# Two transformer layers on one core: one tile back to the plain product, some queries moved into the first tile, and new queue orders

## The chip, the cores and the metric

One core of a Trainium2 chip runs the kernel. The metric is the device time of one execution in microseconds (us); lower is better. The kernel has five instruction queues that matter here: TensorE (PE), VectorE (DVE), ScalarE (ACT), GpSimd (POOL) and SyncE (SP), which issues all transfers.

## The reference

Two layers, each a linear-attention block and an MLP, on 2048 tokens of width 512, in float32. Both layers use the same weights.

```
def _A_ref(x, wqkv, w_phi, wo):            # H = 32 heads of Dh = 16
    qkv = (x @ wqkv) -> q, k, v            # per head
    pq = q @ w_phi[h];  pk = k @ w_phi[h]
    phi_q = concat(softmax(pq), softmax(-pq))   # 32 features a head
    phi_k = concat(softmax(pk), softmax(-pk))
    kv = sum over s of phi_k^T v;  z = sum over s of phi_k
    o = (phi_q kv) / (phi_q z + 1e-6)
    return o @ wo

def _B_ref(x, w1, w2):                     # 512 -> 1792 -> 512
    return maximum(x @ w1, 0) @ w2

for each of two layers:
    x = x + _A_ref(layernorm(x), wqkv, w_phi, wo)
    x = x + _B_ref(layernorm(x), w1, w2)
```

## The kernel before, in words

**Numbers.** Every operand of a large product is split into two float16 halves, high and low, and each product of float32 matrices is three float16 matmuls (high by high, high by low, low by high: `PAIRS`). The weights are scaled, split once and stay on the chip.

**Chunks and tiles.** The 2048 tokens are 16 chunks of 128 (`NCH`) and 8 tiles of two chunks (`TT = 256`, `NT = 8`).

**The front of a layer.** For each chunk: normalise and transpose (`front_norm`, giving `xT`), the keys (`pk`, then the feature map: maxima and minima, differences, exponentials, sums and a product, over DVE, ACT and POOL), the values (`pv`), and `gather`, which adds to the state `kv`. The queries (`query`, `pq`, 12 matmuls) are copied from the bank to `qs` by ACT and stored in `q_dram`. Chunks that are not `direct` store `xT` in `xt_dram`, and their query loads it again as `xq`: in layer 0 the chunks 6 to 15, in layer 1 the chunks 2 to 15. For layer 1 the front of most chunks lies among the tiles of layer 0.

**The opening of a layer** (`opening`). Once `kv` is complete: `summary` makes the right-hand side `rhs`; then for the two chunks of tile 0 the numerators (`pn`), their transposes (`turn`, `tr_o`, `oT`), the projection back (`pw`), the second normalisation (`back_norm`, `tr_b`, `yT`). The queries that are left are emitted here in bank `h`, which has two buffers, in the order of emission; the hidden products of the tiles use bank `h` after them.

**A tile** (`tile_steps`) has seven steps, each for 256 of the 1792 hidden columns. In a step stand the hidden product (`ph`), the activation to `h`, and the output product (`py`) of a step three before it. Among the steps stand, by the table that `sides` makes, the work for later tiles: `look` loads a chunk's query again (`ql`), makes its feature map (`p_q`, last on POOL at L685) and turns it by a transposing transfer on SP (`pT`, L550); `numerators`, `turn`, `back_project` and the normalisation follow a few steps later. They use bank `n`, which has two buffers.

**Plain and by seven.** A hidden step in the plain form (`hidden`, L1308) is 24 matmuls of 256 columns. By seven (`hidden_by_seven`, L1232) it is a scheme of Strassen's kind: seven products instead of eight, 42 matmuls of 128 columns, between which ACT takes three copies `sn` out of the bank (L1245) and DVE makes two adds (L1251, L1256). It needs sums of the rows, made on POOL by `norm_by_seven` (four differences at L958, spreads at L539) and turned by `turn_by_seven` into the place of a weight that is free, and sums of the first weight's blocks. These, seven of them, are made in layer 0 by `sums_of_weight`: 4 loads, 4 operations on POOL (L1105), one on ACT (L1095), one on DVE (L1099), two stores to `s_dram`; each step by seven loads one again as `s` (L1190, 512 KB). `SEVEN` names the tiles by seven of each layer: in layer 0 the tiles 1 to 7, in layer 1 all. `SECOND` names those whose output product goes by seven too (layer 1, tiles 2 to 7); it needs the sums of the second weight, made in layer 0 by `sums_of_second` and loaded from `t_dram` by `load_seconds` into the places of `Wq`, `Wv`, of two more buffers `xT` and of `v`.

**What sets the order.** The program emits tasks with their dependences; buffers of one tag are given out in order of emission. Each of the five queues then has an order written out as a string in `ORDER`: a digit says how many of the tasks still waiting, in order of emission, are passed over. The numbers at `add` are a planner's durations; with the strings in place they don't change what each queue runs, only the order in which the program is written down.

Of the kernel before, what the change touches and what calls it, by code (L numbers as in the profile page):

```python
# [14 lines left out]
ALU = mybir.AluOpType  # L15
# [7 lines left out]
NCH = S // P  # L23
# [6 lines left out]
SEVEN = (range(1, NT), range(NT))  # L30
# [25 lines left out]
        "031110020100990377022b4448012284015183101480220822085130061820310G3003C306207232035q1061013510gg30e20c00"  # L56
        "a00071000020020100000137110001145021373012330201111111190000800000mp00000000p000000000000d00h0l000000000"
        "0000b000000000b0000011111110000000020000000000300030000000000000000050005d00b00f000000000b0000a000008000"
        "0000600000000000000000111100000300030000000000000007a00gg000j00m000000000g000000000000000490000000000000"
        "00000001111116110000300000000000000000003000020007060b00e0000d0000000f0000500000000000000000000011111111"  # L60
        "000011120000000000000000036000b0000000000011111122201122012223333344444444033344444444444444440333333302"
        "222222g2222222222201111111112211112222223331223333333333344444444403333344402222225222222i222l220n111111"
        "110000h00000000000000000242232322000f0010bb0aa008830605003106070009b000000000000000011011111122202222220"
        "1111000000002000001111100001100111111111100000g000g0000000000p0r0000000000p00000000000s00000000000L0000K"
        "00000000V000V0000000000000000000000000000000000000000000m000000000r000000P0000000000I000000V0000000R0000"
        "0000R0000000000000000000000000000000A000Z2000000000000000000000J000000000000000000000000E0000D000I000000"
        "0000000000000000A00000000000000000000000000E00000000000w0000000000000000000w0000000000p0000t000000000000"
        "000000p0000000000000000000000000000000000000000000000000000000000000000000000000000000000000000000000000"
        "0000000000000000000000000000000000000000000000000000000000000000000000000000000000000000000000000000",
    DVE:  # L70
        "331132010000e20c110002110020c0b0k01811922c70h3211d2111e1Yi1c00T0dR44e466f0a5H00ea03302j0w7h1100g00e000j0"
        "d77fb0600ad13ob31000H00efD0G000003H302n0m00k0j1211f111c11f1e1o2131l2p1j122l4f33111222222j1i221f423l11j1i"
        "311122100111525201ee105240311811671605908022040a3902060d2c01a1000013131152131000552772066514112144033908"
        "2060d2c21000700131311524138812007991671194841050b0a09010e020100800601313110102010022330144550440601403a0"
        "92010041b119111051112112112103502325201210504030999908807067b6091514313211100000003022601444133304882225"
        "11101060550036605004403024033101221221000000037302l0k00i00g01e10ci0h0gu01s0r00140000E0MDDK0J01211Z5016Z2"
        "000Y3050200001V02T0211P0115Zc50Za41007171Z2Za01Z80099121ZtZ1Zs91071Zn1908002Zo04dZle11Zi01000ZE0d0ZBZK1b"
        "1ZH01221ZC80Zr160580771g10f11l011i0110111e0d4101101008811h204f110110h11f01200d13229101008471600100b11091"
        "1f0100b01c22a1107110777110110110110100013121011010011010011010001311001101101101100010010",
    ACT:  # L80
        "0033121104642021092110ff5c0ab9a08e1d50551g0o43m0ab0p317m2c62y501C10l150iZjo4tnZf03361Za51108p2hh16ll4184"
        "412d2301gg01200iC081f01b0g0f1302312101aa1e0ee02hyhMx010I101I0q0L1020310203f142c1gb000c80096807o0e69q0300"
        "10l10c10a10811100f2420000001k503h360515003833000421100c122133121070a6004070252429000051230e1440028021142"
        "2201110140303030171151060220030201713013125140a30072114222201122403100a411b06009420620131807105111003022"
        "832253002110000504003032201048403062520120060200205003028222343330022115040034222227780b70a209d9c3bcbbb1"
        "aa008aa88a49730652444401625611373056766676014404377232322023200669100300504060501100044133020m0080102f01"
        "d01m0akaj00h8g8fl8k07ix70vv0003120J101G1R2200B120J14077E0Z370Z175050534334P04Z303214X040373Zs05P56a6Zl05"
        "03Zh444Zu3903322ZnZY0Zm2ZV1000126010ZZ30lZJ100ZW2002ZS2201331214002ZZz2c01ZZc3021ZZq1ZZ7038072d201302u01"
        "a002ZM222004u42021002222103030211302010Zv0220000423830013q02017130401011o3310100303220130200030262040a02"
        "22013026200504h411240020110h330220400200a10200040028221a130221150440001302010030222040022003302040022100"  # L90
        "22201302010022010030222040302003022141020113021000000",
    POOL:
        "1003050930409500905090506y016v90040570b0500790070070b051b0700700101102288827200hhh0g0c10d09bb10002705023"
        "101007j0618811020307210400004744002000111215110014163302221111011102001111104400017360244030010000021011"
        "11050400501302321121112200020011110003020400242321111022001cc4b40302633201003330010000003300000aaaabbm0l"
        "100002100l0k0mm000005p01001k0u0t18U1T00041Z100Y001Zs1100cZn0ZyZy02222201b101110ZZ490ZNd0700910060q500Zy8"
        "0300110n20111001102201110008000Zea000706011o10302031202011i00000220110009000b0591006601000610000f0221101"
        "044d0020d00001110a50006050400060111002211111551311111000000000000010000000000403200000000000001110000000"
        "0",
    SP:  # L100
        "010010002692bf21032470z79b26b1c60250n34303472me834j3j0x2303099r2brcF4066m1226jB30e56S1100308c9hj120823n2"
        "0y1d0110b40022012149111070004763256823g63825266244g02d2066216o1956b7c412b3482051hg443270214619567j59759p"
        "3938175433300662161a6df785436ba1629k7662ae41479022a67cee67b429113330706070a690860032304451bu1n51r411635m"
        "002c32T34fRC24a4w22a77JsF9sa879G196185Ag50eE6L7474hj0s633100a69Ffe9ep1H0c16db9a334H4O5949V27h17mX8628662"
        "50Z0412k21Z2p5141345345002211070g60302i46402221117045002464026222a00045002203323320110400244433001113300"
        "00010",
# [167 lines left out]
def tile_kernel(ctx: ExitStack, tc: tile.TileContext, x_in, wqkv, w_phi, wo, w1, w2, out):  # L274
# [757 lines left out]
    def activate_by_seven(ph, h, n):  # L1032
# [28 lines left out]
        add(POOL, 0.63, first, reads=[r], makes=[rf], after=after_r, **now)  # L1061
        add(POOL, 0.385, lambda: nc.gpsimd.tensor_add(block(1), block(0), rf.ap[:, 1, :]),
            reads=[(rf, None)], writes=[(r, 1)], **now)
        add(ACT, 0.534, hi, reads=[(r, None)], makes=h, **now)
        add(POOL, 0.385, lambda: nc.gpsimd.tensor_sub(rf.ap[:, 2, :], block(2), block(1)),
# [4 lines left out]
        add(POOL, 0.875, lambda: nc.gpsimd.tensor_sub(s.ap[1], rf.ap, s.ap[0]),  # L1070
# [7 lines left out]
    def sums_of_weight(j):  # L1078
# [29 lines left out]
        add(DVE, 1.195, low, reads=[b, s, parts[0]], makes=[parts[1]], lock=True)  # L1108
# [7 lines left out]
    def sums_of_second(j):  # L1116
# [27 lines left out]
        add(DVE, 1.195, low, reads=[b, s, parts[0]], makes=[parts[1]], lock=True)  # L1144
# [16 lines left out]
    def load_seconds():  # L1161

        for j in range(NP):
            if j < 4:
                W, i = (Wq, Wv)[j // 2], j % 2
                seconds[j] = r = Second([lambda h=h, W=W, i=i: flat(W.ap[i])[:, h * 1024:(h + 1) * 1024] for h in range(2)])
                add(SP, 0.47, lambda j=j, W=W, i=i: nc.sync.dma_start(
                    flat(W.ap[i]).rearrange("p (h n) -> p h n", h=2), t_dram[j].rearrange("h p n -> p h n")),
                    reads=[t_res[j]], writes=[(W, f"t{i}"), r], kb=512)
                continue  # L1170
            if j < 6:
# [42 lines left out]
    def hidden_by_seven(l, t, s):  # L1214
# [35 lines left out]
        def plus():  # L1250
            add(DVE, 0.30, lambda: nc.vector.tensor_tensor(at(3), at(1), saved(2), op=ALU.add),  # L1251
                reads=[(ph, 1), (sn, 2)], writes=[(ph, 3)], boost=10 ** 6)

        def both():
            wide = lambda t: t.ap[:, :2 * P]
            add(DVE, 0.43, lambda: nc.vector.tensor_tensor(wide(ph), wide(ph), wide(sn), op=ALU.add),  # L1256
                reads=[(sn, 0), (sn, 1)], writes=[(ph, 0), (ph, 1)], boost=10 ** 6)
# [135 lines left out]
    def leave(l, t, n):  # L1393
# [24 lines left out]
        def plus(x, o, i, y, op, fast, n):  # L1418
            e = DVE if fast else POOL
            add(e, 0.12 + n / 940 if fast else 0.14 + n / 523,  # L1420
# [159 lines left out]
    def sides(l, t):  # L1580
# [41 lines left out]
    def opening(l):  # L1622
# [12 lines left out]
        for c in range(NCH):  # L1635
# [11 lines left out]
        else:  # L1647
            load_seconds()
# [79 lines left out]
    for l in range(2):  # L1728
# [3 lines left out]
        for t in range(NT):  # L1732
            tile_steps(l, t)
# [50 lines left out]
```

## Time and profile before

| | us |
|---|---|
| median of 3 runs | 1000.62 |
| lowest, highest | 999.99, 1003.89 |
| the profiled execution | 1001.27 |
| its span, first to last instruction | 999.5 |
| busy PE, DVE, POOL, ACT in it | 960.4, 675.4, 644.9, 554.7 |
| mean granted clock of TensorE | 0.992 |

Lines of the profile read thus: a group has the line of the code, the engine, the operation, out<-in by the program's names, and the count, then its busy time and the mean of one in ns, then the idle time of its engine just before it and what ended that. A wait has who waited, for what, the total in us, how many times and the longest. A timeline row has the start in us, the length in us, and in brackets an idle time before it. "PE" is the matmuls, "PEld" the loads of weights, "SPq" the queue that issues transfers. The granted clock is 1.00 at full speed.

### The profile page before, as it was taken

Reading aid. Unit: us, or ns where it says so; the run is one execution under the profiler, and the core shown is the slowest. Engines: PE = TensorE matmul, PEld = TensorE weight load, DVE = VectorE, ACT = ScalarE, POOL = GpSimd, SP = SyncE. Lnnn points to the kernel's source line nnn. Section 1 sums busy time; section 2 is a strip of 40 time slices with the busy share of each in tenths; the row PEclk is TensorE's granted clock in tenths of the full one; section 3 lists DMA queues with packets and bytes.
Section 4 is the critical chain, followed back from the end, with each engine's and each line's share of the span. In section 5 each row is a group of like instructions: output and inputs, shape, how many; then the busy total and the mean of one; then the engine's idle time right before and its main releaser. Section 6 shows DMA issues by size and latency. Waiting matters only on the chain.

```text
span 999.5 us, 24139 instructions
## 1 busy us (share of the span) xinstructions
PE 960.4 (96%) x9630; PEld 658.6 (66%) x9630; DVE 675.4 (68%) x1368; ACT 554.7 (55%) x1090; POOL 644.9 (65%) x627
## 2 busy tenths in 40 slices
PE   6999999897999999999999999998999999999997
PEld 5555555574566666656666665546667889888996
DVE  5889899884676777677564556986787644553333
ACT  6898885553454645455334344555455646555553
POOL 1487885787376576657215244475577888898775
PEclk9999999998999999999999999999999999999999
DMA  8365777779769698877846553898999785965540
GB/s 308 136 200 129 193 225 213 176 187 196 198 160 225 180 196 216 189 217 165 182 153 149 177 172 87 268 251 222 233 250 218 204 170 144 207 173 150 155 150 32
DMA packets 257937, 186.30 MB, mean 186 GB/s; under 512 B 186144, under 2 KB 193312, under 8 KB 257824
## 3 DMA queue, kind: packets, MB, share of 16 engines
q1 hardware_dynamic: 257824, 184.76, 70.7%
q8 instruction: 75, 1.23, 0.5%
q14 instruction: 38, 0.31, 0.1%
HBM read 107.51 MB, written 32.51 MB: 140 GB/s over the span
## 4 chain that ended last, share of the span: by engine, by line
PE 74%; DVE 9%; DMA 7%; POOL 5%; ACT 3%; issue 2%; SPq 0%; DVEq 0%; POOLq 0%; ACTq 0%
PE ph L1232 21%; PE py L1340 14%; PE py L1381 8%; PE pk L621 8%; PE pv L621 7%; PE pw L621 6%; PE pq L621 5%; DMA s<-s_dram 2%; PE kv L759 2%; DMA pT<-p_q 2%; PE pn L887 1%; DMA yT<-n_b 1%; POOL p_q L685 1%; DVE fm_q L665 1%; DVE e_q L657 1%
## 5 line engine op out<-in xcount | busy, mean ns | idle before, releaser
L1340 PE MATMUL py<-w,h 128*128 128x512 f16 x840 | 215.2, 381 | 0.0
L1232 PEld LDWEIGHTS <-s 128*128 128x128 f16 x2520 | 163.1, 98 | 43.4 <-issue 5.9
L1245 ACT ACTIVATE sn<-ph 128x128 f32<-128x128 f32 x315 | 86.0, 274 | 180.6 <-PE ph L1232 179.1
L621 PEld LDWEIGHTS <-xT 128*128 128x128 f16 x840 | 80.7, 98 | 91.2 <-DMA xT<-n_a 0.3
L1232 PEld LDWEIGHTS <-w 128*128 128x128 f16 x1890 | 118.9, 98 | 16.8 <-issue 1.6
L1340 PEld LDWEIGHTS <-h 128*128 128x128 f16 x840 | 74.7, 98 | 57.7 <-issue 1.4
L1251 DVE TENSOR_TENSOR ph<-ph,sn 128x128 f32<-128x128 f32 x105 | 31.3, 299 | 118.4 <-PE ph L1232 55.1
L1232 PE MATMUL ph<-yT,s 128*128 128x128 f16 x1260 | 104.9, 219 | 3.6 <-DVE ph L1251 2.9
L674 POOL TENSOR_TENSOR e_k<-e_k,fm_k 128x1024 f32<-128x1024 f32 x30 | 60.8, 2027 | 72.6 <-ACT fm_k L670 72.5
L1232 PE MATMUL ph<-yT,w 128*128 128x128 f16 x1260 | 104.6, 219 | 0.0
L685 POOL TENSOR_TENSOR p_q<-e_q,p_q 128x1024 f16<-128x1024 f32 x32 | 70.9, 2216 | 26.5 <-ACT p_q L681 21.9
L685 POOL TENSOR_TENSOR p_k<-e_k,p_k 128x1024 f16<-128x1024 f32 x30 | 67.5, 2249 | 29.8 <-ACT p_k L681 29.8
L621 PE MATMUL pw<-wo_h,oT 128*128 128x512 f16 x256 | 81.2, 379 | 2.9 <-DVE dn L895 1.7
L1256 DVE TENSOR_TENSOR ph<-ph,sn 128x256 f32<-128x256 f32 x105 | 44.9, 428 | 55.7 <-PE ph L1232 55.0
L621 PE MATMUL pk<-wk_h,xT 128*128 128x512 f16 x256 | 81.4, 379 | 0.0
L621 PE MATMUL pv<-wv_h,xT 128*128 128x512 f16 x256 | 80.9, 379 | 0.0
L674 POOL TENSOR_TENSOR e_q<-e_q,fm_q 128x1024 f32<-128x1024 f32 x32 | 61.9, 1936 | 28.7 <-ACT fm_q L670 28.6
L621 PE MATMUL pq<-wq_h,xq 128*128 128x512 f16 x208 | 65.1, 379 | 1.7 <-ACT e_q L661 1.4
L621 PEld LDWEIGHTS <-oT 128*128 128x128 f16 x384 | 36.4, 98 | 44.2 <-DMA oT<-n_o 2.5
L1000 DVE SCALAR_TENSOR_TENSOR h<-ph,h 128x512 f16<-128x512 f32 x70 | 47.6, 681 | 20.4 <-ACT h L997 19.9
L997 ACT ACTIVATE h<-ph 128x512 f16<-128x512 f32 x70 | 41.4, 591 | 34.5 <-DVE ph L1256 31.8
L539 POOL TENSOR_TENSOR n_a<-xn_a,n_a 128x512 f16<-128x512 f32 x26 | 30.1, 1159 | 42.0 <-ACT n_a L536 27.0
(233 smaller groups left out, 2291.8 us busy)
## 6 DMA issues: line engine op xcount, KB each, us to landing
s<-s_dram SPq DMA_DIRECT2D x105, 512.0 KB, 4.5
q_dram<-qs SPq DMA_DIRECT2D x32, 256.0 KB, 3.4
ql<-q_dram SPq DMA_DIRECT2D x32, 256.0 KB, 4.2
xt_dram<-xT SPq DMA_DIRECT2D x26, 256.0 KB, 3.5
xq<-xt_dram SPq DMA_DIRECT2D x26, 256.0 KB, 3.9
xe<-in_A_x_dram SPq DMA_DIRECT2D x16, 256.0 KB, 4.0
x<-in_A_x_dram SPq DMA_DIRECT2D x16, 256.0 KB, 4.1
x_dram<-x SPq DMA_DIRECT2D x16, 256.0 KB, 3.3
```

Source lines behind the costliest of these rows:

```text
L539: add(POOL, 0.14 + n / 523, lambda: nc.gpsimd.tensor_sub(n16.at()[:, n:], src(), n16.at()[:, :n]), reads=[x], writes=[(n16, "l")])
L621: nc.tensor.matmul(pm.ap, xT.ap[:, a, k, :], W.ap[b][:, k, :], start=(k == 0 and i == 0), stop=(k == KC - 1 and i == 2))
L674: (nc.vector if fast else nc.gpsimd).tensor_tensor(e3, e3, sm.unsqueeze(2).to_broadcast([P, 2 * n, DH]), op=ALU.mult)
L685: (nc.vector if fast else nc.gpsimd).tensor_sub(p16.ap[:, 1, cols], ef, p16.ap[:, 0, cols])
L997: nc.scalar.activation(h[0].ap, at(), AF.Relu)
L1000: add(DVE, 0.607, lambda: nc.vector.scalar_tensor_tensor(h[1].ap, at(), 0.0, h[0].ap, op0=ALU.max, op1=ALU.subtract), reads=[ph, h[0]], wr ...
L1232: nc.tensor.matmul(at(r), weight_of(i, b, kk, s, summed), rows_of(y, i, a, kk), start=(first and kk == 0 and n == 0), stop=(kk == 1 and n ...
L1245: nc.scalar.activation(saved(i), at(2), AF.Copy)
L1251: add(DVE, 0.30, lambda: nc.vector.tensor_tensor(at(3), at(1), saved(2), op=ALU.add), reads=[(ph, 1), (sn, 2)], writes=[(ph, 3)], boost=10 ...
L1256: add(DVE, 0.43, lambda: nc.vector.tensor_tensor(wide(ph), wide(ph), wide(sn), op=ALU.add), reads=[(sn, 0), (sn, 1)], writes=[(ph, 0), (ph ...
L1340: nc.tensor.matmul(py.ap, h[a].ap.rearrange("p j t -> p (j t)")[:, cols], W2.at(b, fs[j], slice(0, D)), start=(s == j == k == 0), stop=(s ...
L1381: nc.tensor.matmul(py.ap[:, 256 * r:256 * r + 256], left[a], right[b], start=(s == 0 and r == 0 and k == 0), stop=(last and k == 2), skip_ ...
```

## The change

It has five parts.

1. `SEVEN` for layer 0 begins with tile 2: tile 1 takes the plain hidden product, and its normalisation the plain form.
2. The sums of the first weight are made at other steps: three in tile 0 and four in tile 1 instead of four and three.
3. `KEPT = (3, 4)`: the last three queries of layer 0 and the last four of layer 1 are no longer in the opening but at index 1 of the first steps of tile 0, in bank `n` instead of `h`.
4. `load_seconds` in layer 1 is emitted before tile 1 instead of in the opening, and the seven loads go to the places in another order: `Wv` takes 0 and 1, the buffers `v` take 2, `xT` takes 3 and 4, `Wq` takes 5 and 6.
5. All five strings of `ORDER` are replaced, and some durations of the planner: six of POOL are longer, two of DVE (L1099 and its like) are longer, two of DVE in the product by seven are shorter.

```
-SEVEN = (range(1, NT), range(NT))
+SEVEN = (range(2, NT), range(NT))
+KEPT = (3, 4)
...
     def load_seconds():
         for j in range(NP):
-            if j < 4:
-                W, i = (Wq, Wv)[j // 2], j % 2
+            if j in (0, 1, 5, 6):
+                W, i = (Wv, j) if j < 2 else (Wq, j - 5)
...
-            if j < 6:
+            if j > 2:
                 bufs = [tiles(fr, "xT", [P, 2, KC, P], F16, f"second_{j}_{h}") for h in "hl"]
...
         if l == 0 and t < 2:
-            for j, s in enumerate((1, 3, 5, 5) if t == 0 else (0, 1, 2)):
-                put0(s, 2, sums_of_weight, j + 4 * t)
+            for j, s in enumerate((2, 3, 5) if t == 0 else (1, 2, 3, 4)):
+                put0(s, 2, sums_of_weight, j + 3 * t)
+        if t == 0:
+            for i in range(KEPT[l]):
+                put(i, 1, query, NCH - KEPT[l] + i, "n")
...
-        for c in range(NCH):
+        for c in range(NCH - KEPT[l]):
             if not (direct(l, c) if l == 0 else c < CPT):
                 query(l, c, "h")
...
             for i in range(2):
                 W2.split(i)
-        else:
-            load_seconds()
...
         for t in range(NT):
+            if l == 1 and t == 1:
+                load_seconds()
             tile_steps(l, t)
...
-        add(POOL, 0.63, first, reads=[r], makes=[rf], after=after_r, **now)
+        add(POOL, 0.69, first, reads=[r], makes=[rf], after=after_r, **now)
...
-        add(DVE, 1.195, low, reads=[b, s, parts[0]], makes=[parts[1]], lock=True)
+        add(DVE, 1.4, low, reads=[b, s, parts[0]], makes=[parts[1]], lock=True)
```

The strings of `ORDER` are not shown. The one of PE has 1395 digits instead of 1452.

More of the change, by code (lines that the diff above doesn't have):

```diff
@@ L55 @@
     PE:
[L56 to L65, printed above, removed]
@@ new lines @@
+        "02000000010131004110000320041520100414004035010134017802884107126203401404413302222333331222222333033333"
+        "33302220100000000111222000000000600900000005000000001111122222222211122222201111122233333022222200000000"
+        "00111222010002017000900000000030000001111122222222211122222222222333403333333333022222222333033022222244"
+        "44403030010000111011122222022222222222122222222222333444444444444444444455566666666888880788888999aaabbb"
+        "bbcccc0b0aaaaaab0aaaaaaaaaaaaaa0990880706055500333333333333333022222333252222222233322223330223333333333"
@@ L1069, in activate_by_seven @@
         add(ACT, 0.42, hi_sums, reads=[(rf, None)], makes=[s], after=after_s, **now)
-        add(POOL, 0.875, lambda: nc.gpsimd.tensor_sub(s.ap[1], rf.ap, s.ap[0]),
+        add(POOL, 0.92, lambda: nc.gpsimd.tensor_sub(s.ap[1], rf.ap, s.ap[0]),
             reads=[(rf, None), (s, None)], writes=[(s, "l")], **now)
@@ L1143, in sums_of_second @@
         add(ACT, 1.052, hi, reads=[b, s], makes=[parts[0]])
-        add(DVE, 1.195, low, reads=[b, s, parts[0]], makes=[parts[1]], lock=True)
+        add(DVE, 1.4, low, reads=[b, s, parts[0]], makes=[parts[1]], lock=True)
         for h in range(2):
@@ L1250, in plus @@
         def plus():
-            add(DVE, 0.30, lambda: nc.vector.tensor_tensor(at(3), at(1), saved(2), op=ALU.add),
+            add(DVE, 0.27, lambda: nc.vector.tensor_tensor(at(3), at(1), saved(2), op=ALU.add),
                 reads=[(ph, 1), (sn, 2)], writes=[(ph, 3)], boost=10 ** 6)
@@ L1255, in both @@
             wide = lambda t: t.ap[:, :2 * P]
-            add(DVE, 0.43, lambda: nc.vector.tensor_tensor(wide(ph), wide(ph), wide(sn), op=ALU.add),
+            add(DVE, 0.40, lambda: nc.vector.tensor_tensor(wide(ph), wide(ph), wide(sn), op=ALU.add),
                 reads=[(sn, 0), (sn, 1)], writes=[(ph, 0), (ph, 1)], boost=10 ** 6)
```

83 lines of the change are left out of this document (43 added, 40 removed).

## The prediction

> **What bounds the kernel now.** I read the page first (busy shares), then the windows of 25 us and 5 us, the waits, and the timeline of the stretches where TensorE (PE) is not full.
>
> ```profile
> span 999.5 us, 24139 instructions
> ...
> PE 960.4 (96%) x9630; PEld 658.6 (66%) x9630; DVE 675.4 (68%) x1368; ACT 554.7 (55%) x1090; POOL 644.9 (65%) x627
> ```
>
> PE is busy for 960.4 of 999.5 us, so a change pays only by taking work from PE, by closing some of the other 39.1 us, or by raising the clock. The windows say where those lie (columns: stretch, its length, busy time of PE, PEld, DVE, ACT, POOL, granted clock, DMA share, GB/s):
>
> ```profile
> 0.00:25.00 25.00, 16.50 (x108) 13.73 (x109) 14.48 (x42) 16.89 (x37) 4.70 (x17) 1.00 0.85 307
> ...
> 75.00:100.00 25.00, 25.00 (x197) 12.71 (x194) 23.38 (x34) 22.00 (x29) 17.98 (x12) 1.00 0.53 130
> ...
> 175.00:200.00 25.00, 20.11 (x201) 13.96 (x200) 20.80 (x42) 13.26 (x20) 19.66 (x15) 0.93 0.71 176
> ...
> 225.00:250.00 25.00, 17.98 (x187) 12.23 (x186) 12.31 (x31) 8.88 (x19) 19.77 (x21) 0.87 0.90 195
> ...
> 975.00:1000.00 25.00, 17.66 (x211) 16.08 (x208) 8.81 (x16) 8.27 (x20) 12.61 (x18) 0.95 0.07 25
> ```
>
> The start (8.5 us idle) and the end (7.3 us) are not touched. 4.9 us are idle at 175 to 200, the opening and first tile of layer 0, and 7.0 us at 225 to 250, where its second tile begins. The waits of PE, for 160 to 300 us and for 600 to 720 us:
>
> ```profile
> PE pn L887 <- DMA pT<-p_q: 5.8, 2, 4.9
> PE tr_b L565 <- ACT xn_b L599: 3.2, 2, 1.8
> PE pw L621 <- DVE dn L895: 1.7, 1, 1.7
> PE ph L1232 <- DMA s<-s_dram: 1.2, 1, 1.2
> PE tr_o L565 <- DVE o L898: 0.8, 1, 0.8
> ...
> PE pq L621 <- ACT e_q L661: 1.4, 1, 1.4
> ...
> PE pq L621 <- DMA xq<-xt_dram: 0.3, 1, 0.3
> ```
>
> So the dearest wait is that of the numerators for a turned feature map (pT) in tile 1. On GpSimd and on the DMA queue it looks so (start, us, operation):
>
> ```profile
> 236.67 0.73 POOL L1105 TENSOR_TENSOR sums<-sums 128x256 f32<-128x256 f32 x1
> 237.35 0.73 POOL L958 TENSOR_TENSOR xn_b<-xn_b,ts 128x256 f32<-128x256 f32 x1
> 238.04 2.13 POOL L685 TENSOR_TENSOR p_q<-e_q,p_q 128x1024 f16<-128x1024 f32 x1
> ...
> 240.38 2.91 SPq L550 DMA_TRANSPOSE pT<-p_q  x1
> ...
> 245.39 1.54 PE L887 MATMUL pn<-rhs,pT 128*128 128x68 f16 x24 [4.89 <-DMA pT<-p_q]
> ```
>
> The reader is to see a queue, not a slow transfer: the feature map's last GpSimd step stands behind the sums of the first weight (L1105) and the differences for the seven products (L958); only then can its DMA start, and PE waits 1.2 us more for the next sum of weights (s), the row of the waits.
>
> **The change, part by part.**
>
> (a) Layer 0's tile 1 by the plain product. A plain step is 24 matmuls of 256 columns, a step by seven 42 of 128:
>
> ```profile
> L1308 PE MATMUL ph<-yT,w x216: 218/272/311, 182.5 to 218.3; 128*128 128x256 f16 x60, 128*128 128x128 f16 x48
> ...
> 211.86 2.78 PE L1308 MATMUL ph<-yT,w 128*128 128x256 f16 x24
> 214.48 1.46 PE L1340 MATMUL py<-w,h 128*128 128x512 f16 x6
> ...
> 231.60 0.50 PE L1232 MATMUL ph<-yT,s 128*128 128x128 f16 x6
> 231.93 0.50 PE L1232 MATMUL ph<-yT,w 128*128 128x128 f16 x6
> ...
> s<-s_dram SPq DMA_DIRECT2D x105, 512.0 KB, 4.5
> ```
>
> Start to start, 214.48 - 211.86 = 2.62 us against 7 x (231.93 - 231.60) = 2.31 to 2.35 us (0.33 is rounded), so 0.27 to 0.31 us more in each of 7 steps: +1.9 to +2.2 us on PE, which nothing hides; I take +1.9. What goes with it: 7 of the 105 loads of s; in norm_by_seven and turn_by_seven four differences on GpSimd (0.73 us each by the row of L958 above) and two spreads with their two turns; 21 copies sn on ScalarE and 14 adds on VectorE. None is on the path where PE is full; they stand in front of pT where it is not.
>
> (b) The sums of the first weight go from 4 in tile 0 and 3 in tile 1, wanted from tile 1's first step, to 3 and 4, wanted from tile 2's. Their GpSimd work is the largest group in 160 to 275 us:
>
> ```profile
> L1105 POOL TENSOR_TENSOR sums<-sums 128x256 f32<-128x256 f32 x28 | 23.3, 832 | 2.7 <-DMA sums<-in_B_w_dram 1.8
> ...
> SPq L550 <- POOL sums L1105: 26.8, 9, 6.2
> ```
>
> The second row is the DMA queue's own wait list for 180 to 260 us: turns (L550) held in order for 26.8 us while the sums ran. The work stays; its due time moves a tile later (tile 0 has its hidden products from 182.5 to 218.3 us, row of L1308), so it can be put behind pT. I count no term for it by itself: it is why (a)'s and (c)'s cover can be used.
>
> (c) Three queries of layer 0 leave the opening for steps 0 to 2 of tile 0, in the other bank. One is 2.59 us on PE:
>
> ```profile
> 129.74 2.59 PE pq L621 x12
> ...
> 25.00:160.00 135.00, 135.00 (x965) 71.55 (x964) 120.06 (x211) 116.93 (x177) 99.91 (x65) 1.00 0.62 180
> ```
>
> Each takes along its load of xq and the store of qs on SP, and the copy to qs on ScalarE; what it stores is read back tiles later. It joins two lines: the buffers xq, which the halves of the weight's sums hold until they are stored, and bank n, which it holds through its copy. PE waited for xq 0.3 us in all before, and 1.4 us once for a bank whose copy stood behind an exponential (rows above, 600 to 720); so between 0 and 1.4 us for each of the seven moved queries, 9.8 us at most. I take 0, as the load can be issued early and the copy is one instruction; the end is kept for the range. 7.8 us of PE work move from a stretch in which PE has no gap to one in which it has them. pT is late by 5.8 us in all; with 7.8 us more work ahead of those numerators on PE, and less ahead of their turn on GpSimd (a, b), I take the 5.8 us to go, and with them the 1.2 us for s (no s is read in tile 1 any more): -7.0 us. The wait of pw for dn (1.7 us, at 192, inside tile 0) can have a query in front of it: -1.7 us. The gap at 178 to 182 (tr_b, 3.2 us) can't, as step 0 comes after it, and stays.
>
> Is the opening shorter by those 7.8 us? In 25 to 160 us VectorE was busy for 120.1 us; in 127.2 us that would be 94%. At 75 to 100 us it ran at 23.38 of 25 (94%) and PE had no gap. So the cover may be just enough; between none lost and all 7.8 us lost I take 1.5 us: +1.5.
>
> (d) The clock. After the gap at 240 to 245 the matmuls were slow:
>
> ```profile
> 240.00:245.00 5.00, 0.49 (x9) 0.32 (x6) 3.24 (x4) 3.15 (x6) 4.54 (x5) 0.83 1.15 232
> 245.00:250.00 5.00, 3.42 (x38) 2.94 (x39) 1.61 (x6) 0.38 (x2) 3.05 (x5) 0.50 1.03 269
> 250.00:255.00 5.00, 5.00 (x30) 2.66 (x28) 3.24 (x8) 2.01 (x4) 1.06 (x2) 0.65 0.56 124
> ...
> 180.00:185.00 5.00, 3.66 (x40) 3.65 (x41) 4.12 (x8) 3.41 (x5) 3.21 (x2) 0.69 1.01 249
> ```
>
> Lost: 0.49 x 0.17 + 3.42 x 0.50 + 5.00 x 0.35 = 3.5 us, which go with the gap: -3.5. The 3.66 x 0.31 = 1.1 us after the gap at 178 to 182 stay with it.
> The Trainium skill ("TensorE: Matmul & The Clock Gate", Part 1: The HAM clock gate) says that the array drops to half rate after an idle window of about 3.4 us and needs about as long of work to come back. By that page, as an estimate, one such gap costs some 1.7 us, and the sum would end 1.8 us higher. The 5 us rows show more after the 4.89 us gap, and a drop at 180 where no gap was over 1.82 us, which the page's window would not give; the rows decide.
>
> (e) Layer 1: four queries to steps 0 to 3 of its first tile, and the loads of the second weight's sums (t_dram) behind them, since two lie in Wq.
>
> ```profile
> 606.00:640.00 34.00, 34.00 (x245) 17.71 (x244) 27.20 (x51) 16.93 (x27) 13.64 (x9) 1.00 0.64 184
> 640.00:676.00 36.00, 33.30 (x251) 16.96 (x248) 30.32 (x62) 18.90 (x29) 22.71 (x17) 1.00 0.97 252
> 676.00:700.00 24.00, 21.11 (x239) 14.97 (x238) 16.13 (x37) 12.00 (x28) 13.35 (x10) 1.00 0.81 224
> 700.00:725.00 25.00, 25.00 (x269) 16.62 (x266) 18.79 (x46) 12.79 (x27) 14.43 (x13) 1.00 1.10 238
> ```
>
> The opening, 606 to 676, has 67.3 us of PE work and 57.5 of VectorE's. Without 4 x 2.59 = 10.4 us PE has 56.9, so VectorE sets it: at the 94% above 61.2 us, 8.8 less than 70. Tile 0 gains 10.4 us of work and loses its 2.9 us of gaps (24.00 - 21.11), which the queries can fill. Together -8.8 + 10.4 - 2.9 = -1.3 us. Bounds: the opening not shorter at all, +7.5; as short as PE allows, 56.9, -5.6.
>
> (f) New orders for all five queues, and costs that only feed the planner. Where the order of the rest of the work changes I can't price it from rows; the waits there, outside the places above, are some 5 us, of which I take nothing, and I leave the same on the other side.
>
> Sum: +1.9 - 7.0 - 1.7 + 1.5 - 3.5 - 1.3 = -10.1 us. The profiled execution took 1001.27 us (span 999.5), so 991.2; the median of the runs is 0.65 us lower, so 990.5.
>
> **The rivals.**
>
> 1. The openings don't get shorter (slower). The queries were the cover of a chain on VectorE, and the chain ends where it did; the moved PE work is added behind it. For: VectorE was busy for 89% and 84% in the rows of 25 to 160 and 640 to 676 us, where looks and weight splits stand in one queue with that chain. Against: PE had no gap at all at 94%. Price: 7.8 instead of 1.5 in layer 0, +7.5 instead of -1.3 in layer 1, which is 15.1 more, 1005.6; with one clock loss of the size of (d), 3.5, as the new gaps are long, 1009. It decides from the point where VectorE's share of an opening stays what it was, 89% in layer 0 and 57.5 of 70 us in layer 1.
>
> 2. The late transfers only move. The pT wait reappears in tile 1, or, as four of the seven sums are now made in tile 1, at tile 2's first s; and of t_dram's loads 1.25 MB (three of 256 KB, one of 512) were issued before 700 us and now come after, at the 238 GB/s of the row 700 to 725 5.3 us of transfer where the DMA share is 1.10 already.
>
> ```profile
> L1181 SPq DMA_DIRECT2D v<-t_dram x2: 479/524/570, 661.1 to 677.9; - x2
> L1181 SPq DMA_DIRECT2D second_h<-t_dram x2: 422/610/797, 678.5 to 706.4; - x2
> ...
> L1167 SPq DMA_DIRECT2D wq_l<-t_dram x1: 529/529/529, 692.7 to 692.7; - x1
> ```
>
> If the 5.8 us and their 3.5 us of clock stay, 990.5 + 9.3 = 999.8; if only the 5.3 us are added, 995.8. No change. Against it: the row 700 to 725 has no PE gap in spite of its share.
>
> 3. The new order also closes the other gaps: tr_b and tr_o (4.0 us) with their 1.1 us of clock, the 1.5 us of (c), layer 1 at its lower bound (4.3 more): 990.5 - 10.9 = 979.6. For: that much is idle. Against: these are chains, and PE needs something ready in them.
>
> **How the numbers follow.** Chances: the forecast (985 to 995.6) 0.50, rival 3 0.16, rival 2 0.20, rival 1 0.14. What a measurement can tell here is 0.5%, 5 us, so faster is below 995.6: 0.50 + 0.16 = 0.66, same 0.20, slower 0.14. The predicted time is the forecast's, 990.5; its own range is 985 to 995.6. Rival 3's time and rival 1's without the clock loss bound the whole range: 980 to 1005, which leaves out about 1 in 10 on each side.
>
> **What would show it.** In the new profile: no wait of pn for pT over 1 us between 200 and 300 us and a granted clock of 1.00 in the rows there (c, d); PE L1308 x384 instead of x216 and s loaded 98 times (a); the first step of tile 0 of layer 0 earlier by some 6 us than 182.5 and that of layer 1 earlier against the kernel's own 606 by some 9 us (c, e); DVE at over 90% in the openings. Wrong would make me: PE gaps with VectorE as releaser in 130 to 180 or 620 to 670 us (rival 1), waits for s at tile 2 or for t_dram's tiles after 725 (rival 2).

## The result and the profile after

| | us |
|---|---|
| changed kernel, median of 4 runs (lowest to highest) | 989.03 (988.47 to 990.29) |
| kernel before, on the same chip, median of 4 runs | 1002.25 (999.99 to 1008.23) |
| ratio, 95% interval | 0.9861 [0.9814, 0.9907] |
| the profiled execution of the changed kernel, its span | 990.29, 988.6 |

The changed kernel is faster by 1.4%, more than the 0.5% that can be told from no change. In the code after the change each line number is one less than before: L1307 is the plain hidden product, L1231 the one by seven.

First the page of the changed kernel.

```profile
span 988.6 us, 23825 instructions
...
PE 956.5 (97%) x9504; PEld 654.5 (66%) x9504; DVE 675.3 (68%) x1354; ACT 546.9 (55%) x1067; POOL 637.9 (65%) x621
...
s<-s_dram SPq DMA_DIRECT2D x98, 512.0 KB, 4.4
```

And from a list of one line's instructions the plain product (count, shortest, median and longest in ns, first and last start).

```profile
L1307 PE MATMUL ph<-yT,w x384: 216/272/273, 174.3 to 269.6; 128*128 128x256 f16 x144, 128*128 128x128 f16 x48
```

The change did what it says: 126 matmuls fewer (7 steps of 24 for 7 of 42), 384 plain ones, 98 loads of s. Now the windows that answer to those of before.

```profile
25.00:160.00 135.00, 134.76 (x991) 71.98 (x990) 118.94 (x212) 114.62 (x174) 97.00 (x65) 1.00 0.59 172
160.00:200.00 40.00, 36.56 (x350) 23.83 (x349) 36.27 (x72) 23.05 (x33) 25.10 (x17) 1.00 0.75 193
...
225.00:250.00 25.00, 25.00 (x194) 15.59 (x192) 14.02 (x36) 11.46 (x17) 23.08 (x25) 1.00 0.78 189
...
600.00:700.00 100.00, 95.91 (x851) 56.52 (x850) 77.56 (x155) 50.99 (x96) 56.65 (x42) 1.00 0.87 235
```

PE is full where 7.0 us were idle (225 to 250), at a clock of 1.00. The stretch around the first tile's start has come forward, so for it the window is 160 to 200 us in both kernels; in the kernel before it reads:

```profile
160.00:200.00 40.00, 34.34 (x342) 22.20 (x339) 34.92 (x72) 21.37 (x31) 28.74 (x22) 0.96 0.70 188
```

There 3.4 us are idle (40.00 - 36.56) where 5.7 were. Idle PE went from 39.1 us (999.5 - 960.4) to 32.1 (988.6 - 956.5). Busy PE fell by 3.9 us. Before, PE worked for 3.41 and 6.96 us in the two stretches in which the clock stood at 0.50 (the last section shows how they are found), so half of that, 5.2 us, was lost; after, it had no such work, so the work itself grew by 1.3. Together -7.0 - 5.2 + 1.3 = -10.9 us of span. The waits of PE from 150 to 310 us, all that are left:

```profile
PE tr_b L564 <- ACT xn_b L598: 1.2, 1, 1.2
PE ph L1307 <- ACT yT L569: 0.7, 1, 0.7
PE tr_o L564 <- DVE o L897: 0.7, 2, 0.3
PE tr_o L564 <- DVE dn L894: 0.5, 1, 0.5
PE ph L1307 <- DVE yT L573: 0.5, 1, 0.5
```

No wait for pT, s or dn in front of pw is among them. The queue, in the timeline of the same places as before:

```profile
226.59 5.20 POOL L684 TENSOR_TENSOR p_q<-e_q,p_q 128x1024 f16<-128x1024 f32 x2
231.75 0.55 POOL L601 TENSOR_TENSOR stat_a<-stat_a,nhalf 128x1 f32<-128x1 f32 x1
232.27 2.21 POOL L1104 TENSOR_TENSOR sums<-sums 128x256 f32<-128x256 f32 x3
...
231.81 2.96 SPq L549 DMA_TRANSPOSE pT<-p_q  x1
```

and the numerators of 180 to 260 us, from the list of instructions that touch pT:

```profile
L886 PE MATMUL pn<-rhs,pT x120: 192/194/198, 185.3 to 241.1; 128*128 128x68 f16 x120
```

The last GpSimd step of both maps of the pair now stands directly ahead of three operations of the sums; before, an operation of the sums and a difference stood directly ahead of the late one. The last turn is issued at 231.81 (240.38 before), and the last of the numerators starts at 241.1, well behind it.

Where does each layer end? The last hidden product by seven of a layer is the best mark (the second row of each pair is for layer 1):

```profile
L1232 PE MATMUL ph<-yT,w x168: 219/219/219, 500.3 to 606.6; 128*128 128x128 f16 x168
...
L1232 PE MATMUL ph<-yT,w x672: 218/219/219, 676.4 to 986.0; 128*128 128x128 f16 x168
```

for the kernel before, and for the changed one

```profile
L1231 PE MATMUL ph<-yT,w x132: 219/219/219, 504.8 to 595.0; 128*128 128x128 f16 x132
...
L1231 PE MATMUL ph<-yT,w x672: 217/219/219, 652.4 to 975.0; 128*128 128x128 f16 x168
```

Layer 0 ends 606.6 - 595.0 = 11.6 us earlier. Before, 12 matmuls of values (pv) more and 6 of the output product (py) fewer stood ahead of that mark, which makes 6 of 128x512, 1.3 us by the row of a query (2.59 / 12 each). So layer 0 is 10.3 us shorter and layer 1 (379.4 + 1.3 against 380.0) 0.7.

### The profile page after: what moved, and what is told of

Its sections match the earlier page's. It is cut to its first block, busy times and chain, and to the rows that moved or that the text cites. A ratio compares the mean times of both kernels' runs of the same rounds, so it can differ in the third digit from the quotient of the medians.

```text
span 988.6 us, 23825 instructions
## 1 busy us (share of the span) xinstructions
PE 956.5 (97%) x9504; PEld 654.5 (66%) x9504; DVE 675.3 (68%) x1354; ACT 546.9 (55%) x1067; POOL 637.9 (65%) x621
## 4 chain that ended last, share of the span: by engine, by line
PE 78%; DVE 7%; DMA 6%; POOL 3%; ACT 3%; issue 3%; SPq 0%; DVEq 0%; ACTq 0%; POOLq 0%
PE ph L1231 19%; PE py L1339 15%; PE py L1380 9%; PE pk L620 7%; PE pv L620 7%; PE pw L620 7%; PE pq L620 5%; PE ph L1307 4%; PE kv L758 2%; PE pn L886 2%; DMA oT<-n_o 1%; DMA ql<-q_dram 1%; DMA pT<-p_q 1%; DMA q_dram<-qs 1%; POOL p_q L684 1%
## 5 line engine op out<-in xcount | busy, mean ns | idle before, releaser
L1339 PE MATMUL py<-w,h 128*128 128x512 f16 x840 | 212.9, 379 | 0.0
L1231 PEld LDWEIGHTS <-s 128*128 128x128 f16 x2352 | 151.4, 98 | 37.5 <-issue 7.3
L1244 ACT ACTIVATE sn<-ph 128x128 f32<-128x128 f32 x294 | 80.2, 273 | 138.5 <-PE ph L1231 136.9
L1231 PEld LDWEIGHTS <-w 128*128 128x128 f16 x1764 | 110.8, 98 | 17.6 <-DVE h L999 2.7
L1250 DVE TENSOR_TENSOR ph<-ph,sn 128x128 f32<-128x128 f32 x98 | 29.3, 299 | 111.1 <-PE ph L1231 53.3
L1231 PE MATMUL ph<-yT,s 128*128 128x128 f16 x1176 | 97.6, 219 | 5.3 <-DVE ph L1250 2.9
L1231 PE MATMUL ph<-yT,w 128*128 128x128 f16 x1176 | 97.6, 219 | 2.1 <-DVE h L999 1.8
L673 POOL TENSOR_TENSOR e_q<-e_q,fm_q 128x1024 f32<-128x1024 f32 x32 | 64.9, 2030 | 35.7 <-ACT fm_q L669 35.7
L1255 DVE TENSOR_TENSOR ph<-ph,sn 128x256 f32<-128x256 f32 x98 | 41.9, 428 | 46.1 <-PE ph L1231 45.3
L620 PEld LDWEIGHTS <-xq 128*128 128x128 f16 x312 | 29.9, 98 | 35.5 <-DMA xq<-xt_dram 0.9
```

The lines of the kernel that those rows point to most:

```text
L620: nc.tensor.matmul(pm.ap, xT.ap[:, a, k, :], W.ap[b][:, k, :], start=(k == 0 and i == 0), stop=(k == KC - 1 and i == 2))
L673: (nc.vector if fast else nc.gpsimd).tensor_tensor(e3, e3, sm.unsqueeze(2).to_broadcast([P, 2 * n, DH]), op=ALU.mult)
L1231: nc.tensor.matmul(at(r), weight_of(i, b, kk, s, summed), rows_of(y, i, a, kk), start=(first and kk == 0 and n == 0), stop=(kk == 1 and n ...
L1244: nc.scalar.activation(saved(i), at(2), AF.Copy)
L1250: add(DVE, 0.27, lambda: nc.vector.tensor_tensor(at(3), at(1), saved(2), op=ALU.add), reads=[(ph, 1), (sn, 2)], writes=[(ph, 3)], boost=10 ...
L1255: add(DVE, 0.40, lambda: nc.vector.tensor_tensor(wide(ph), wide(ph), wide(sn), op=ALU.add), reads=[(sn, 0), (sn, 1)], writes=[(ph, 0), (ph ...
```

## The experiments

The experiments fall into three sets; in each, the kernel before ran between the others on the same chip (medians 1002.22, 1003.74 and 1003.5 us), and the ratios are to it. Two theories of the gap at 240 us stood against each other first: that pT is late by its place in the queues (A), or that the tile by seven itself is too tight (B).

**again**: the kernel before, unchanged.

> The kernel before, unchanged, for a second trace. If the late feature map belongs to the kernel, the wait of pn for pT at the start of the second tile of layer 0 (4.9 us) and the clock of about 0.5 behind it are there again, and the time is that of before within 0.3%. If they belong to the one execution, the wait is under 2 us here, and the sum of the prediction rested on a chance.

1.0007 [0.9987, 1.0027]. The gap is a property of the kernel: the longest wait for pT is 5.2 us (4.9 in the first profile). The clock loss after it was 3.0 us in this execution (half of the 5.96 us of work at 0.50), and none came at 180.

**late_map_first**: the late map's steps passed forward in three queues (parts of the strings of `ORDER`).

```
 ACT  -  ...1503h360515003833000...        +  ...1503h3g6051500333000...
 POOL -  "101007j0618811020307210400...     +  "101007j7i01881102030210400...
 SP   -  ...9111070004763256...            +  ...9111070a00463256...
```

> The kernel before with four instructions moved in its queues: the feature map of chunk 7 of layer 0 has its last step on ScalarE (high), its last two chunks' steps on GpSimd (low of chunks 6 and 7) and its turn on SP ahead of the normalisation for tile 2 and the sums that stood in front. Theory A, the queue: the late pT was only a matter of what stood in front of it; the 5.8 us of waits and the 3.5 us of clock go, the normalisation and the sums come some 4 us later and are not missed: 8 us faster (6 to 10). Theory B, the structure: the work in front is needed there, so the wait passes to s, to the rows of tile 2 or to a later map, and the gain is under 2 us.

0.999 [0.9972, 1.0008]. The waits of PE, 160 to 300 us:

```profile
PE ph L1232 <- DMA s<-s_dram: 4.1, 2, 3.3
PE pw L621 <- DMA oT<-n_o: 3.0, 1, 3.0
PE tr_b L565 <- ACT xn_b L599: 2.4, 2, 1.4
PE ph L1232 <- ACT sn L1245: 1.9, 2, 1.3
PE tr_o L565 <- DVE o L898: 0.8, 1, 0.8
```

The wait for pT is gone and its time stands at s, oT and sn. Theory A falls for this order: another place in the queues only hands the delay on.

**filler**: 20 matmuls of 128x512 whose result nobody reads, ahead of the late numerators.

```
+        if l == 0 and t == 1:
+            pb = bank("kv0", "filler")
...
+                for i in range(FILL):      # FILL = 20
+                    nc.tensor.matmul(pb.ap, Wk.ap[0][:, 0, :P], Wk.ap[0][:, 0, :], start=True, stop=True)
```

> The kernel before with 20 matmuls of 128x512 that nobody reads (20 x 0.216 = 4.3 us) put on TensorE in front of the numerators of chunk 7, in a bank that is free there; they fill the 4.9 us gap. Nothing else changes. By the rows of the granted clock (0.50 and 0.65 behind the gap) 3.5 us come back: 0.3 to 0.4% faster. By a window of some 3.4 us at half rate it would be 1.7 us. If the low clock has another cause than the gap, nothing.

0.9974 [0.9955, 0.9992]: 2.6 us faster with 4.3 us (20 x 2.59 / 12) of useless work, the interval 0.8 to 4.5. The clock after the gap:

```profile
240.00:245.00 5.00, 3.65 (x37) 1.86 (x35) 3.08 (x5) 1.36 (x4) 4.84 (x5) 1.00 1.02 188
245.00:250.00 5.00, 3.54 (x20) 1.90 (x21) 2.14 (x6) 1.31 (x2) 1.11 (x2) 0.70 1.12 303
250.00:255.00 5.00, 5.00 (x38) 2.88 (x36) 3.89 (x10) 2.52 (x5) 2.45 (x3) 0.96 0.57 183
```

The loss in these rows is 3.54 x 0.30 + 5.00 x 0.04 = 1.3 us, against 3.5 in the prediction's rows (1.7 by the recorded clock of the last section). So the time of a gap's slow clock is real, and cover on PE buys part of it back. This one profile took 1001.64 us (the median is 999.41) and has a second loss, at 421 us, that the kernel before doesn't have there. Over all executions the mean granted clock agrees: its median is 0.997 in 12 of filler and 0.993 in 28 of the kernel before.

**before_new_order**: the kernel before with all five strings found anew by a search over the planner's durations.

> The kernel before, the same instructions, with all five queue orders searched anew from its own (single tasks moved, a planner's durations as the measure, two more sets of durations beside the kernel's). If the new orders alone bring the gain of the change, 8 us or more here; if the tile by the plain product and the moved queries bring it, under 4 us.

1.0082 [1.0049, 1.0114]. A searched order is 8 us worse than the one written down, with the idle time spread out: 6.06 us at 160 to 200, 1.82 at 200 to 225, 3.82 at 225 to 300, 6.66 at 300 to 500. The wait for pT is down to 0.5 us in 160 to 300, with the same instructions; but PE waits there 2.9 us for oT and 1.8 for s. So this order too hands the delay on, as late_map_first does. Orders found by search must be compared with each other, not with an order that was there.

**sums_light**: the kernel before without the 28 operations on GpSimd of the sums.

```
-            add(POOL, 0.686, lambda o=o, x=x, y=y, f=f: nc.gpsimd.tensor_tensor(f32()[:, o], ...
+            add(POOL, 0.686, lambda: None, writes=[b])
```

> The kernel before without the 28 operations on GpSimd that make the sums of the first weight (the halves are made from the blocks as loaded, so the hidden products of the tiles by seven are of other weights); all transfers, conversions and orders stay. 28 x 0.83 = 23.3 us of GpSimd's time leave 165 to 265 us. If GpSimd's queue is what made pT and s late, the waits of the second tile go with it and 7 us of idle time and 3.5 of clock with them: 8 to 10 us faster. If the transfers are (SP's queue and the DMA share of 0.9 there), less than 3 us.

1.0023 [1.0004, 1.0041], and the gap stays. The wait of PE, 160 to 300 us:

```profile
PE pn L887 <- DMA pT<-p_q: 5.6, 2, 5.1
```

and the late map in the timeline:

```profile
235.26 1.05 ACT L681 ACTIVATE p_q<-e_q 128x1024 f16<-128x1024 f32 x1
...
237.89 2.13 POOL L685 TENSOR_TENSOR p_q<-e_q,p_q 128x1024 f16<-128x1024 f32 x1
238.06 3.10 SPq L1091 DMA_DIRECT2D sums<-in_B_w_dram  x4
...
241.26 2.95 SPq L550 DMA_TRANSPOSE pT<-p_q  x1
```

The prediction read GpSimd as the head of the queue. With those operations gone the map's step on GpSimd still comes at 237.89: its ScalarE half comes only at 235.26, behind copies sn and the halves of the normalisation by seven, and two differences follow it on GpSimd (236.40 and 237.21). It ends at 240.02, and the turn still waits until 241.26 behind four loads on SP. Read so, the chain goes through ScalarE's order, GpSimd's differences and SP's order; that the sums' operations are not its limit is shown.

**The parts apart.** The next five are the changed kernel with queries put back into the openings or not; the stretches of the order that an edit touches were searched anew, and `after_searched` is the control with no edit.

**after_searched**: only strings of `ORDER` in the openings and first tiles.

> The control for the two others: the changed kernel with nothing undone, its order searched again in the same stretches and by the same measure. If the search by itself costs nothing, the changed kernel's time, 988 to 991; what it has more is the price of the search, to be taken off the two others.

**kept1_only**: `-KEPT = (3, 4)` `+KEPT = (0, 4)`; layer 0 searched.

> The changed kernel with the three queries of layer 0 back in the opening, in bank h (KEPT = (0, 4)); the tile by the plain product, the sums' steps and layer 1 as changed. The order is the changed kernel's, with the tasks of layer 0's opening and its first two tiles searched again for the moved queries. If those queries were the cover that the late feature maps needed, some of the waits come back: 3 to 7 us slower than the changed kernel, 992 to 996. If the plain tile and the later sums were enough, 987 to 991.

**none_kept**: `+KEPT = (0, 0)`; both layers searched.

> The changed kernel with none of the seven queries moved (KEPT = (0, 0)), its order searched again in the two openings and the tiles behind them. The sum of the prediction puts the queries of layer 1 at 1.3 us and counts on those of layer 0 for the cover: 994 to 999. If the moved queries are worth little and the plain tile is what counts: 988 to 993.

**kept0_only**: `+KEPT = (3, 0)`; layer 1 searched.

> The changed kernel with layer 1's four queries put back into its opening; layer 0 stays as it is, and the order of layer 1's opening and first two tiles is searched anew, as in the control whose order alone was searched anew (0.9918). Theory: layer 1's queries carry 4 to 5 us and layer 0's almost nothing, so this is 0.4 to 0.5% over the control, 0.995 to 0.997 of the kernel before, and PE idles some 4 us more than the changed kernel's 4.1 us in 600 to 700 us. Rival, the terms of the prediction: layer 1's queries carry 1.3 us, so 0.993, with some 1 us more idle there.

**after_again**: no edit.

> The changed kernel once more, unchanged, beside the two others on one chip. Both theories: 0.984 to 0.989 of the kernel before; its lead of some 5 us over the control with a searched order comes back.

| kernel | queries moved | ratio | last hidden product of layer 0, of layer 1 | difference |
|---|---|---|---|---|
| after_again | 3, 4 | 0.9859 [0.9835, 0.9883] | 594.9, 973.7 | 378.8 |
| after_searched | 3, 4 | 0.9918 [0.9892, 0.9943] | 599.7, 978.1 | 378.4 |
| kept1_only | 0, 4 | 0.9907 [0.9884, 0.993] | 598.4, 977.6 | 379.2 |
| kept0_only | 3, 0 | 0.9967 [0.9949, 0.9985] | 595.8, 985.0 | 389.2 |
| none_kept | 0, 0 | 0.9957 [0.9938, 0.9976] | 594.6, 982.1 | 387.5 |

The work ahead of layer 0's mark is nearly the same: after_searched, kept0_only and none_kept have 6 matmuls of the output product fewer there (1.3 us), and none_kept 24 short ones of the state more. The rows behind kept0_only, then none_kept:

```profile
L1231 PE MATMUL ph<-yT,w x132: 218/219/220, 506.4 to 595.8; 128*128 128x128 f16 x132
...
L1231 PE MATMUL ph<-yT,w x672: 218/219/220, 679.5 to 985.0; 128*128 128x128 f16 x168
```

```profile
L1231 PE MATMUL ph<-yT,w x132: 219/219/219, 505.0 to 594.6; 128*128 128x128 f16 x132
...
L1231 PE MATMUL ph<-yT,w x672: 216/219/314, 672.8 to 982.1; 128*128 128x128 f16 x168
```

Layer 0 ends at 594.6 and 598.4 without its three queries moved, at 594.9 to 599.7 with them: no difference beyond what orders make. Nor does the time show one: kept1_only is at 0.9907, its control after_searched at 0.9918. none_kept has the same plain tile and later sums and none of the queries, and no wait for pT from 160 to 300 us (kept1_only has 1.2 us at 191, in tile 0, and 0.5 later):

```profile
PE tr_b L564 <- ACT xn_b L598: 1.2, 1, 1.2
PE tr_o L564 <- DVE dn L894: 1.0, 2, 0.5
PE ph L1231 <- ACT sn L1244: 0.8, 1, 0.8
PE tr_o L564 <- DVE o L897: 0.7, 2, 0.3
PE ph L1231 <- DVE h L999: 0.6, 1, 0.6
```

What the plain tile and the later sums carry, with no query moved on either side, is read from none_kept against before_new_order, both with searched orders: 0.9957 against 1.0082, and layer 0's mark at 594.6 against 611.2, of which at most 2.6 us is work that stands on the other side of the mark. The prices of the two searches, 0.6 and 0.8%, explain little of that.

So theory B stands, with an open end: all five have the plain tile and the later sums together, and no run separates these two.

Layer 1 takes 378.4 to 379.2 us with its four moved and 387.5 to 389.2 without; the time is in 600 to 700 us, first kept0_only, then none_kept (the changed kernel's row is above):

```profile
600.00:700.00 100.00, 89.30 (x748) 50.08 (x747) 78.27 (x158) 48.47 (x87) 54.54 (x38) 0.98 0.81 211
```

```profile
600.00:700.00 100.00, 91.95 (x768) 53.20 (x766) 77.47 (x161) 51.56 (x92) 55.97 (x39) 0.98 0.89 232
```

10.7 and 8.1 us idle against 4.1. But the kernel before, with its own order and no query moved, took 380.7 (above), again 382.3 (987.2 - 606.2 + 1.3), and before_new_order 384.0 (993.9 - 611.2 + 1.3); the 1.3 is added for the work that these have ahead of the mark. Beside the changed kernel's 380.0 and after_again's 378.8, layer 1's four queries and what goes with them are worth 0.7 to 3.5 us against that order and some 4 to 11 against a searched one; in time, 0.5% (none_kept against kept1_only) to 1.1% (kept0_only against after_again). I had expected 0.995 to 0.997 for kept0_only, which came, with some 4 us more of idle PE, where 6.6 came. Its order in layer 0 was the good one of the changed kernel, though, so the price is higher than the 0.49% that its ratio shows against after_searched. Why no searched order without the moved queries came to the 380.7 is open.

none_kept, at 0.9957, lies 0.39% over its control, 3.9 us. With the prediction's terms it would have been 1.3 for layer 1 and up to 7.2 for layer 0 (7.0 + 1.7 - 1.5); by the marks all of it is layer 1's.

**seven_kept**: tile 1 of layer 0 by seven again with the early sums, queries moved; all strings searched.

```
-SEVEN = (range(2, NT), range(NT))
-KEPT = (3, 4)
+SEVEN = (range(1, NT), range(NT))
+KEPT = (2, 4)
...
-            for j, s in enumerate((2, 3, 5) if t == 0 else (1, 2, 3, 4)):
-                put0(s, 2, sums_of_weight, j + 3 * t)
+            for j, s in enumerate((1, 3, 5, 5) if t == 0 else (0, 1, 2)):
+                put0(s, 2, sums_of_weight, j + 4 * t)
```

> The other half alone: layer 0's tile 1 by seven products again with the sums of the first weight as early as before (4 and 3), two queries of layer 0 and four of layer 1 in the first tiles' steps, all orders searched anew as in the kernel before with a new order (1.0082). Theory: the by-seven chain of tile 1 makes the gap and queries ahead of it are no cover, so pT, s or what replaces them still costs 4 to 7 us of idle PE in 225 to 300 us, and only layer 1's 4 to 5 us are gained: about 1.004 of the kernel before. Rival, the prediction's step (c): the two queries' 5.2 us lie ahead of the late numerators and cover them; idle PE in 225 to 300 us is under 2 us, and with 5.2 us, the clock's 3 and layer 1's 4 the time is about 0.996.

1.0083 [1.0062, 1.0104]: both missed. Idle PE at 225 to 300 us is 2.7 us, between the two, but 7.8 us are idle at 160 to 200 with the clock at 0.91, and layer 1 takes 390.9 us (604.8 to 995.7; 382.7 in before_new_order). There PE waits (600 to 720 us):

```profile
PE pq L622 <- DMA xq<-xt_dram: 4.2, 3, 2.3
PE ph L1233 <- DMA yT<-n_b: 2.3, 1, 2.3
```

The three waits for xq lie between 639 and 650 us, ahead of layer 1's first hidden product at 674.1. Whether the queries that wait are moved ones the trace doesn't tell; kept0_only, with none of layer 1's moved, has a wait for xq of 2.5 us too. Under searched orders the moved queries without the plain tile and the later sums gain nothing: 1.0083, against 1.0082 for before_new_order. In layer 0 the mark stands at 604.8 with the same count of matmuls ahead as before_new_order's, which is at 611.2. That is 6.4 us less; but two orders of one program differ there by 6.1 (594.9 in after_again, 599.7 with 1.3 us less work ahead in after_searched). So whether two queries cover anything for a tile by seven is not shown.

## Why the prediction was right

The time was forecast at 990.5; the median is 989.03, the profiled execution 990.29, 11.0 us below before's where the sum said 10.1. By layers it is near (layer 0: 1.9 - 7.0 - 1.7 + 1.5 - 3.5 = -8.8, measured -10.3; layer 1: -1.3, measured -0.7). But part of the hit is luck. The sum started from 1000.62, a median of three that lies below the later medians of the same kernel (1002.22 to 1003.74); against runs on the same chip the change is worth 13.2 us (1002.25 to 989.03) and 14.4 (1003.5 to 989.11). And not every step carries its own term.

- (a) +1.9: PE's work at full clock grew by 1.3 us, and the counts are as said. Its main effect was booked elsewhere: none_kept shows that the plain tile, with the later sums and their order, closes the gap without the queries.
- (b) "can be put behind pT": seen in the timeline. That their GpSimd work was what held pT is wrong (sums_light).
- (c) the step that failed, though its number came out: -7.0 and -1.7 were credited to the queries as cover, the first together with less work ahead of the turn on GpSimd. The waits for pT, for s and of pw for dn went, but in none_kept they went without any query. +1.5 for the opening is not seen: from 25 us to the first hidden product PE idled for 3.2 us (174.3), against 4.0 before (182.5). VectorE stood at 118.94 of 135 us, 88%, not over 90%; by rival 1's own point that is a share that stayed, yet the gaps of rival 1 didn't come, so the share did not decide. The first step of tile 0 came at 174.3, 8.2 us earlier where 6 were said.
- (d) -3.5: 5.2 us less clock loss between the two profiles, 3.5 behind the gap as said and 1.7 at 180 (1.1 by its row), which was to stay. Between executions of the same kernel this differs (5.2 and 3.0), and filler gained 2.6 us [0.8, 4.5], which leaves both the rows' 3.5 and the 1.7 of the estimate from the Trainium skill possible for its gap. What sets the loss is in the last section.
- (e) -1.3: -0.7 by the marks of the two profiles, -3.5 by those of again and after_again (382.3 and 378.8), so the size is not known better than that. Both halves were under-sized and nearly cancel: the first step of layer 1 came 57.4 us after layer 0's mark (652.4 - 595.0), 1.3 of them the work that came over, against 69.8 (676.4 - 606.6), so 13.7 earlier where 8.8 were said, and the tiles gave back 13.0 (322.6 against 309.6) where 7.5 were said. VectorE did not set the opening at 94%, as (e) had it: its busy time there fell with PE's, its share is 83% before and after, and PE is what is full (56.61 of 57.40 us). First the opening before, then after:

```profile
606.60:676.40 69.80, 67.10 (x484) 34.26 (x482) 57.92 (x113) 35.82 (x56) 36.37 (x25) 1.00 0.81 218
```

```profile
595.00:652.40 57.40, 56.61 (x418) 29.46 (x415) 47.40 (x93) 28.57 (x47) 25.03 (x18) 1.00 0.71 212
```

- (f) 0 for the orders: under-sized. The same program with a searched order in a few stretches is 0.6% slower (0.9918 against 0.9859), and the kernel before 0.8%; the order is of the size of the parts.
- Rival 2 (the waits only move) is what happened in late_map_first, not in the change. Rival 3 came in part: tr_b and tr_o fell from 4.0 to 2.4 us and the clock loss at 180 went, while 1.2 us of waits for yT are new.

## What to carry to other kernels

A wait that ends on a transfer may be a chain through several in-order queues. Removing the largest load on one of them left the wait where it was (sums_light), passing the transfer forward moved it along (late_map_first), and the stage with less work of its own no longer had it (here with 1.3 us more on PE). A gap that goes may be credited to its cover or to the removal of its cause; here it went without the cover, so test the parts one by one before crediting either. And compare edits under orders found in the same way, since the order alone moved the time by 0.6 to 0.8%.

## What the runs showed of the clock

The length of a gap alone does not decide whether the clock drops, nor how much is lost. The traces record the granted clock with the start and the length of each stretch. In all 13 profiles it is 1.00 or 0.50 from 25 us on, each stretch at 0.50 before the end of the program is 3.41 us long or two or three times that, and within one execution all their starts and ends lie on one grid of 3.41 us steps. In another execution the grid lies elsewhere. Windows cut on it show this, first for the big gap of the kernel before, then for a gap of 1.97 us in filler (418.95 to 420.92), then for one of 3.04 us in late_map_first (190.58 to 193.62):

```profile
239.88:243.29 3.41, 0.61 (x11) 0.44 (x8) 1.84 (x4) 3.10 (x6) 2.95 (x5) 1.00 1.23 238
243.29:253.54 10.25, 6.96 (x51) 4.59 (x52) 5.71 (x12) 2.19 (x5) 4.76 (x5) 0.50 0.86 210
```

```profile
417.63:421.05 3.42, 1.45 (x19) 0.98 (x17) 1.22 (x5) 0.15 (x1) 3.28 (x5) 1.00 1.28 184
421.05:424.46 3.41, 3.41 (x28) 2.33 (x27) 0.97 (x4) 0.94 (x3) 0.91 (x1) 0.50 1.04 296
424.46:427.87 3.41, 3.41 (x22) 1.74 (x21) 0.86 (x2) 1.56 (x4) 1.78 (x2) 1.00 0.03 12
```

```profile
188.17:191.58 3.41, 2.41 (x54) 2.29 (x51) 3.31 (x6) 1.74 (x4) 3.04 (x3) 1.00 0.91 76
191.58:194.99 3.41, 1.37 (x7) 0.66 (x8) 3.31 (x8) 1.37 (x3) 2.89 (x3) 1.00 0.68 169
194.99:198.40 3.41, 3.41 (x18) 1.52 (x17) 2.13 (x5) 1.21 (x2) 3.41 (x2) 1.00 0.43 116
```

The shorter gap lies in one step and is followed by half clock; the longer one is shared out between two steps and is not. Over all profiles, from 32 to 980 us: behind each of the 11 steps at full clock in which PE was busy for at most 1.28 of the 3.41 us the clock fell, behind none with 1.72 or more; of the 8 between 1.35 and 1.62 us 5 were followed by a fall and 3 not, so PE's busy time is not the whole rule. Where the grid lies is chance as far as these runs show, and so is whether a gap of 2 to 3 us costs anything.

The Trainium skill ("TensorE: Matmul & The Clock Gate", Part 1: The HAM clock gate) has an idle window of about 3.4 us. The length agrees with the 3.41 us of these traces, but the step need not be idle: in filler PE was busy for 1.45 us of it. So the drop at 180 that the prediction held against that page does not contradict the window's length: no gap there was over 1.82 us, but in the step from 178.44 to 181.86 PE was busy for only 1.18 us. What a drop costs is half of PE's work in the stretch. That is 1.5 to 1.7 us where the stretch is one step long, as the estimate from that page has it, 2.2 and 2.7 in sums_light and seven_kept (two steps) and 3.0 and 3.5 in again and the kernel before (three steps). So the prediction's 3.5 for its gap was right, for this execution.
